# The second network's clamp, square, maximum and rounding issued ahead of the last block product's addition, and no conversions in the first unit

## The chip, the cores and the metric

The kernel runs on one core of one Trainium2 chip. The core has five engines that work side by side, each through its own queue in order: TensorE (PE; its weight loads are shown as PEld), VectorE (DVE), ScalarE (ACT), GpSimd (POOL) and SyncE (SP), which here mostly issues transfers. An engine waits for another through semaphores. The metric is the time of one execution on the device in microseconds, lower is better.

## What is computed

Attention without a softmax, whose output goes through two networks of two layers each:

```python
def _attn_ref(u, v, z):                       # u, v: 2 x 3008 x 256, z: 2 x 3008 x 64
    scores = (1.0 / S) * np.matmul(z, z.transpose(0, 2, 1))
    attn = np.maximum(scores, 0.0) ** 2
    return u * np.matmul(attn, v)

def _moe_ref(x, w_in, w_out):                 # x: 6016 x 256, w_in: 256 x 2048, w_out: 2048 x 256
    h = x @ w_in
    return (h - np.tanh(h)) @ w_out

def _moe2_ref(x, w_in, w_out):                # the same shapes
    h = x @ w_in
    neg, pos = h <= -1.0, h >= 1.0
    g = np.where(pos, h, np.where(neg, 0.0, (h + 1.0) ** 2 / 4.0))
    return g @ w_out
```

The second network's g is the maximum of h and (c/2 + 1/2)^2, where c is h clamped to -1 to 1. The inputs of the networks' weights are 64-bit floats, which the kernel converts itself.

## The kernel before

**Numbers in two parts.** Matrix operands are cut into a rounded part (hi) and the rest (lo); a product of two matrices is three matmuls, hi by lo, lo by hi and hi by hi.

**Stages.** Attention takes some 480 us. Between its steps the weights are converted (`convert`, `posts`, driven by `work`), stored in DRAM (`packed`) and later fetched 512 KB at a time. Then come the units of the first network (net 0, 48 of them), those of the second (net 1, 40), and an end stage for the last tokens of the second network. A unit is one slice of 256 hidden channels (f, 8 of them) for a strip of tokens (s: up to 1024, in two halves of 512).

**One unit** (`Unit.emit`). The first layer is a 2 by 2 block product, done with seven block products instead of eight (`mult`, L557, three matmuls each). They collect in three PSUM banks Y, X and V; intermediate sums in Y are copied out by ScalarE (`snap`: m1, u2, u3) before the next product is added into the same bank. VectorE adds them up (`add`, L496) to the hidden values: half A (`ha`: m1 + X, then u3 + V) and half B (`hb`: a copy of Y by ScalarE, and u2 + V). Each half then goes through the steps of `Half`:

- `first` is the tanh on ScalarE in net 0 (L509) and the clamp on VectorE in net 1 (L511);
- `square` (L516, ScalarE) is there in net 1 alone;
- `value` (L519, VectorE) is the subtraction in net 0 and the maximum in net 1, into `ta` or `tb`;
- `round` (L493 by `copy`, ScalarE) makes the rounded part `gha` or `ghb`;
- `rest` (L530, VectorE) makes the remainder `gla` or `glb`.

The second layer (`parts`, L576) takes these as operands, 24 matmuls a unit. It runs one unit later: while unit u does its first layer, `one`, `two` and `three` of the unit ahead of it, p, stand between the products. `one` needs gha, `two` gla and ghb, `three` glb. So a unit has 21 + 24 = 45 matmuls.

**What sets the order.** Nothing is scheduled: each engine takes its instructions in the order in which `emit` writes them. In net 1 the order before is: round of p's A and clamp of p's B ahead of m1; p's A rest and B square; m1 + X; p's B value; B's rounding; a filling step; u3; u3 + V; **then** p's B rest; a filling step; the clamp of the own A; the products into Y and V; the copy for B; the square of A; the addition for B; the value of A.

**Filling steps.** `fill` is called twice in a unit (once in the first one). It takes the next step of the splitting of the following strip's tokens (`x_steps`, in units f = 2 to 5: subtractions L433, roundings L452, remainders L468), or the turning of finished output (L688), and when there is none, a piece of weight conversion (`work`).

**The last unit of a strip.** `empty`, called at the end of the following unit, copies the four finished banks out; in net 1 all four copies are ScalarE's.

Of the kernel before, what the change touches and what calls it, by code (L numbers as in the profile page):

```python
# [29 lines left out]
def attention_then_two_ffn(  # L30
# [452 lines left out]
    def fill():  # L483

        if fills:
            for fn in fills.pop(0):
                if fn is not None:
                    fn()
        else:
            work(CONVERT[1])  # L490

    def copy(out_, in_):
        nc.scalar.activation(out=out_, in_=in_, func=AF.Copy)  # L493

    def add(out_, x, bank):
        nc.vector.tensor_tensor(out=out_, in0=x, in1=bank, op=ALU.add)  # L496
# [46 lines left out]
    class Unit:  # L543
# [57 lines left out]
        def emit(self, p, att=None):  # L601

            w = self.w
            one, two, three = p.parts_list if p else ([], [], [])
            Y = self.bank()
            self.mult(Y, A11, "b11", True)
            if p and p.net == 1:
                p.A.round()
                p.B.first()
            m1 = self.snap("m1", Y)  # L610
            X = self.bank()
            self.mult(X, A12, "b21", True)
            if p:
                p.A.rest()
                p.B.first() if p.net == 0 else p.B.square()
            self.A = Half(self.net, w, "a")
            add(self.A.h[:, 0, :w], m1, X[:, :w])
            V = self.bank()
            self.mult(V, S1, "t1", True)
            self.mult(Y, S2, "t2")  # L620
            u2 = self.snap("u2", Y)
            if p:
                p.B.value()
            for fn in one:
                fn()
            if att:
                att[0]()
            if p:
                p.B.round()
                fill()  # L630
            self.mult(Y, S3, "t3")
            u3 = self.snap("u3", Y)
            if p and p.net == 0:
                p.B.rest()
            add(self.A.h[:, 1, :w], u3, V[:, :w])
            if p and p.net == 1:
                p.B.rest()
            for fn in two:
                fn()
            if att:  # L640
                att[1]()
            fill()
            if self.net == 1:
                self.A.first()
            self.mult(Y, A22, "t4")
            self.mult(V, S4, "b22")
            self.B = Half(self.net, w, "b")
            if self.net == 0:
                self.A.first()
                copy(self.B.h[:, 1, :w], Y[:, :w])  # L650
                self.A.value()
                add(self.B.h[:, 0, :w], u2, V[:, :w])
            else:
                copy(self.B.h[:, 1, :w], Y[:, :w])
                self.A.square()
                add(self.B.h[:, 0, :w], u2, V[:, :w])
                self.A.value()
            for fn in three:
                fn()
            if self.net == 0:  # L660
                self.A.round()
            if p:
                p.empty()
            self.parts_list = self.parts()
# [58 lines left out]
    def end_s(q):  # L723

        f, c = divmod(q, 2)
        n = SIZES[c]
        xh, xl = xsp[c]
        win = ws[len(units) + f][0]
        banks = [ps_f.tile([P, 512], F32, tag="f", name="h") for _ in range(2)]
        for j in range(2):  # L730
            for k in range(2):
                for i, (wp, x) in enumerate(((0, xl), (1, xh), (0, xh))):
                    nc.tensor.matmul(  # L733
                        banks[j][:, :n], win[wp][:, 2 * k + j, :], x[:, k, :n],
                        start=(k == 0 and i == 0), stop=(k == 1 and i == 2),
                    )
        return banks
# [129 lines left out]
    with tc.manual_schedule():  # L867
# [52 lines left out]
        def work(amount):  # L920

            if not (converts or posts):
                return
            state["credit"] += amount
            if posts:
                cost, fn = posts.pop(0)
                fn()
                state["credit"] -= cost
            while converts and state["credit"] > 0:
                if state["step"] == 0:  # L930
                    next(converts[0])
                elif state["step"] == 4 and len(converts) > 1:
                    next(converts[1])
                state["step"] += 1
                cost = next(converts[0], None)
                if cost is None:
                    converts.pop(0)
                    state["step"] = 1
                else:
                    state["credit"] -= cost  # L940
# [65 lines left out]
        p = None  # L1006
        for i, (net, s, f) in enumerate(units):
# [10 lines left out]
            p = u  # L1018
# [2 lines left out]
        one, two, three = p.parts_list  # L1021
        nq = 2 * NPF
        banks = end_s(0)
        p.A.round()
        p.B.first()
        p.A.rest()
        p.B.square()
# [53 lines left out]
```

## Time and profile before

| | us |
|---|---|
| median of 3 runs (lowest to highest) | 1528.29 (1525.94 to 1530.37) |
| the profiled execution | 1522.68 |
| span in it, first to last instruction | 1520.9 |
| TensorE busy | 1465.9 (96%) |
| VectorE busy | 1264.5 (83%) |
| ScalarE busy | 1034.3 (68%) |
| GpSimd busy | 54.5 (4%) |

The end of a matmul is modelled in these profiles, so that a busy TensorE is not one at its peak; weight loads are the closer measure, as each matmul has one (80% of the span). Times in the trace are counted from the start of the span. In the rows, "<-" in square brackets names what ended an engine's idle time ahead of the instruction, and how long that was.

### The profile page before, as it was taken

What the parts mean: (1) busy time and instruction counts of PE and PEld (TensorE: products, weight loads), DVE (VectorE), ACT (ScalarE), POOL (GpSimd) and SP (SyncE); (2) the same over time, 40 slices, a digit from 0 to 9 for tenths busy, and PEclk for the clock granted to TensorE, in tenths of its full rate; (3) what the DMA queues carried; (4) which work ended last, traced back from release to release, by engine and by line L of the source; (5) the groups of instructions that cost most, each with busy time, mean ns of one, the idle gap of its engine ahead of it and who ended that gap; (6) DMA issues with size and microseconds to landing.
All of it is one profiled execution on the core that took longest, in us unless ns stands there. A gap on an engine that the chain in (4) does not pass through costs nothing.

```text
span 1520.9 us, 22304 instructions
## 1 busy us (share of the span) xinstructions
PE 1465.9 (96%) x8653; PEld 1223.2 (80%) x8653; DVE 1264.5 (83%) x1510; ACT 1034.3 (68%) x1249; POOL 54.5 (4%) x69
## 2 busy tenths in 40 slices
PE   9999999999999999999999999989988899899998
PEld 6888998888888888888888889867776777677897
DVE  8999888988897888888989898777777777777775
ACT  8877778877776677676767767655656556565543
POOL 0110000000110000000000010000000000000000
PEclk9999999999999999999999999999999999999999
DMA  6333335233335657584746575645435645346361
GB/s 153 84 98 98 98 98 115 64 94 95 97 105 178 235 200 252 170 303 135 287 148 247 184 252 206 235 171 192 137 107 161 206 166 165 104 141 211 125 194 25
DMA packets 202170, 240.80 MB, mean 158 GB/s; under 512 B 130000, under 2 KB 139088, under 8 KB 202064
## 3 DMA queue, kind: packets, MB, share of 16 engines
q1 hardware_dynamic: 200864, 239.12, 48.2%
q8 instruction: 67, 1.10, 0.3%
q10 hardware_dynamic: 1200, 0.26, 0.1%
q14 instruction: 39, 0.32, 0.1%
HBM read 195.69 MB, written 43.65 MB: 157 GB/s over the span
## 4 chain that ended last, share of the span: by engine, by line
PE 72%; DVE 12%; ACT 9%; issue 5%; DMA 1%; SPq 0%; ACTq 0%; DVEq 0%
PE acc L335 24%; PE acc L576 21%; PE m L557 17%; PE sc L287 6%; DVE ta L519 3%; ACT ta L516 3%; PE h L733 3%; DVE ha L496 2%; DVE tb L519 2%; DVE glb L530 2%; ACT gha L493 2%; PE acc L769 1%; PE acc L790 1%; DVE ta L511 1%; ACT u L493 1%
## 5 line engine op out<-in xcount | busy, mean ns | idle before, releaser
L335 PE MATMUL acc<-hi,v 64*128 64x512 f32 (+1 forms) x2256 | 282.3, 383 | 0.0
L335 PEld LDWEIGHTS acc<-hi,v 64*128 64x128 f32 x2256 | 220.3, 184 | 35.6 <-ACT hi L300 0.8
L557 PE MATMUL m<-xht,w 128*128 128x512 f32 (+1 forms) x704 | 216.7, 389 | 0.0
L308 ACT ACTIVATE r<-sc 128x1024 f32<-128x1024 f32 (+1 forms) x143 | 143.6, 1004 | 72.4 <-PE sc L287 71.7
L321 DVE TENSOR_TENSOR lo<-a,hi 128x1024 fp32r<-128x1024 f32 (+1 forms) x143 | 171.6, 1207 | 20.3 <-ACT a L315 17.7
L576 PE MATMUL acc<-ghb,w 128*128 128x512 f32 (+1 forms) x704 | 186.5, 387 | 0.0
L557 PE MATMUL m<-xlt,w 128*128 128x512 f32 (+1 forms) x352 | 141.7, 403 | 46.2 <-ACT m L493 46.0
L576 PE MATMUL acc<-gha,w 128*128 128x512 f32 (+1 forms) x704 | 175.2, 392 | 0.0
L576 PEld LDWEIGHTS acc<-gha,w 128*128 128x128 f32 x704 | 133.9, 190 | 27.9
L335 PE MATMUL acc<-lo,v 64*128 64x512 f32 (+1 forms) x1104 | 153.4, 384 | 1.7 <-DVE lo L321 1.7
L576 PEld LDWEIGHTS acc<-ghb,w 128*128 128x128 f32 x704 | 132.2, 188 | 25.9
L557 PEld LDWEIGHTS m<-xht,w 128*128 128x128 f32 x704 | 132.8, 189 | 24.4
L311 ACT ACTIVATE hi<-r 128x1024 fp32r<-128x1024 f32 (+1 forms) x143 | 149.3, 1044 | 4.2
L530 DVE TENSOR_TENSOR gla<-ta,gha 128x1024 fp32r<-128x1024 f32 (+1 forms) x88 | 106.7, 1213 | 44.7 <-ACT gha L493 44.7
L493 ACT ACTIVATE gha<-ta 128x1024 fp32r<-128x1024 f32 (+1 forms) x88 | 92.6, 1052 | 64.3 <-DVE ta L519 63.5
L519 DVE TENSOR_TENSOR ta<-ha,ta 128x1024 f32<-128x1024 f32 (+1 forms) x88 | 107.0, 1216 | 32.6 <-ACT ta L516 19.4
L493 ACT ACTIVATE u<-m 128x512 f32<-128x512 f32 (+1 forms) x176 | 103.7, 589 | 43.9 <-PE m L557 38.5
L317 DVE TENSOR_TENSOR a<-r 128x1024 f32<-128x1024 f32 (+1 forms) x95 | 114.9, 1210 | 21.4 <-ACT r L308 19.2
L557 PEld LDWEIGHTS m<-xlt,w 128*128 128x128 f32 x352 | 66.1, 188 | 76.3 <-ACT m L493 63.8
L493 ACT ACTIVATE ghb<-tb 128x1024 fp32r<-128x1024 f32 (+1 forms) x88 | 92.6, 1052 | 47.9 <-DVE tb L519 47.9
L335 PEld LDWEIGHTS acc<-lo,v 64*128 64x128 f32 x1104 | 108.9, 184 | 19.6 <-DVE lo L321 3.2
L493 ACT ACTIVATE hb<-m 128x512 f32<-128x512 f32 (+1 forms) x88 | 52.2, 594 | 102.0 <-PE m L557 100.8
(103 smaller groups left out, 2435.1 us busy)
## 6 DMA issues: line engine op xcount, KB each, us to landing
w<-packed SPq DMA_DIRECT2D x288, 512.0 KB, 5.7
xr<-kept SPq DMA_DIRECT2D x20, 512.0 KB, 7.7
widein<-in_moe_w_in_dram SPq DMA_DIRECT2D x16, 512.0 KB, 5.8
wideout<-in_moe_w_out_dram SPq DMA_DIRECT2D x16, 512.0 KB, 4.2
packed<-phin SPq DMA_DIRECT2D x16, 512.0 KB, 2.8
packed<-plin SPq DMA_DIRECT2D x16, 512.0 KB, 2.9
vraw<-in_v_dram SPq DMA_DIRECT2D x22, 256.0 KB, 3.7
out_dram<-ot SPq DMA_DIRECT2D x88, 64.0 KB, 1.9
```

Source lines behind the costliest of these rows:

```text
L287: nc.tensor.matmul(ps[:, j, :n], zs[b, g][half, x, k0 : k0 + P], q[half, y, :n], start=(k == 0), stop=(k == 2))
L308: nc.scalar.activation(out=r[s], in_=ps[s], func=AF.Relu)
L311: nc.scalar.activation(out=hi[s], in_=r[s], func=AF.Square)
L317: nc.vector.tensor_tensor(out=a[s], in0=r[s], in1=r[s], op=ALU.mult)
L321: tail.append(lambda: nc.vector.tensor_tensor(out=lo[s], in0=a[s], in1=hi.bitcast(F32)[s], op=ALU.subtract))
L335: nc.tensor.matmul(acc[d][h][:, :n], lhsT, g[half, j, :n], start=start, stop=stop)
L493: nc.scalar.activation(out=out_, in_=in_, func=AF.Copy)
L516: nc.scalar.activation(out=self.t[self.s], in_=self.t[self.s], func=AF.Square, scale=0.5, bias=0.5)
L519: nc.vector.tensor_tensor(out=self.t[self.s], in0=self.h[self.s], in1=self.t[self.s], op=ALU.subtract if self.net == 0 else ALU.max,)
L530: nc.vector.tensor_tensor(out=self.lo[self.s], in0=self.t[self.s], in1=self.hi.bitcast(F32)[self.s], op=ALU.subtract)
L557: nc.tensor.matmul(bank[:, : self.w], self.win[wp][:, block, :], xop[self.net, self.s][x][xp], start=start and i == 0, stop=True, skip_gro ...
L576: nc.tensor.matmul(self.acc(d, n)[:, : self.w], self.wout[:, part, j, d * P : (d + 1) * P], g[:, at, : self.w], start=start, stop=stop,)
```

## The change

In the units of net 1, p's B rest is written directly behind B's rounding and the filling step, ahead of the second addition to A; the own A's clamp directly behind that addition, ahead of `two` and of the second filling step; A's square ahead of the copy for B; A's value ahead of the addition for B. The rounding of A stands at the end of its own unit in both networks, and p's clamp of B behind the product A12. In the first unit of all (the one with `att`, net 0) the tanh of A is written ahead of attention's last steps, and the filling step is left out.

```diff
             Y = self.bank()
             self.mult(Y, A11, "b11", True)
-            if p and p.net == 1:
-                p.A.round()
-                p.B.first()
             m1 = self.snap("m1", Y)
             X = self.bank()
             self.mult(X, A12, "b21", True)
             if p:
+                if p.net == 1:
+                    p.B.first()
                 p.A.rest()
                 p.B.first() if p.net == 0 else p.B.square()
...
             if p:
                 p.B.round()
                 fill()
+                p.B.rest()
             self.mult(Y, S3, "t3")
             u3 = self.snap("u3", Y)
-            if p and p.net == 0:
-                p.B.rest()
             add(self.A.h[:, 1, :w], u3, V[:, :w])
-            if p and p.net == 1:
-                p.B.rest()
+            if self.net == 1 or att:
+                self.A.first()
             for fn in two:
                 fn()
             if att:
                 att[1]()
-            fill()
+            if not att:
+                fill()
             if self.net == 1:
-                self.A.first()
+                self.A.square()
             self.mult(Y, A22, "t4")
             self.mult(V, S4, "b22")
             self.B = Half(self.net, w, "b")
-            if self.net == 0:
+            if self.net == 0 and not att:
                 self.A.first()
-                copy(self.B.h[:, 1, :w], Y[:, :w])
-                self.A.value()
-                add(self.B.h[:, 0, :w], u2, V[:, :w])
-            else:
-                copy(self.B.h[:, 1, :w], Y[:, :w])
-                self.A.square()
-                add(self.B.h[:, 0, :w], u2, V[:, :w])
-                self.A.value()
+            copy(self.B.h[:, 1, :w], Y[:, :w])
+            self.A.value()
+            add(self.B.h[:, 0, :w], u2, V[:, :w])
             for fn in three:
                 fn()
-            if self.net == 0:
-                self.A.round()
+            self.A.round()
             if p:
                 p.empty()
...
         nq = 2 * NPF
         banks = end_s(0)
-        p.A.round()
         p.B.first()
```

VectorE, from the second unit of net 1 into the third, in the kernel before (`ha<-u` is the second addition to A, `hb<-u` the addition for B, `ha<-m` the first addition to A of the next unit):

```order
L519 TENSOR_TENSOR tb<-hb,tb 128x1024
L496 TENSOR_TENSOR ha<-u_11097,m 128x512
L530 TENSOR_TENSOR glb<-tb,ghb 128x1024
L511 TENSOR_SCALAR ta<-ha 128x1024
L496 TENSOR_TENSOR hb<-u_11077,m 128x512
L519 TENSOR_TENSOR ta<-ha,ta 128x1024
L511 TENSOR_SCALAR tb<-hb 128x1024
L530 TENSOR_TENSOR gla<-ta,gha 128x1024
L496 TENSOR_TENSOR ha<-m_11145,m 128x512
```

The same place in the changed kernel:

```order
L519 TENSOR_TENSOR tb<-hb,tb 128x1024
L530 TENSOR_TENSOR glb<-tb,ghb 128x1024
L496 TENSOR_TENSOR ha<-u_11099,m 128x512
L511 TENSOR_SCALAR ta<-ha 128x1024
L519 TENSOR_TENSOR ta<-ha,ta 128x1024
L496 TENSOR_TENSOR hb<-u_11077,m 128x512
L511 TENSOR_SCALAR tb<-hb 128x1024
L530 TENSOR_TENSOR gla<-ta,gha 128x1024
L496 TENSOR_TENSOR ha<-m_11143,m 128x512
```

Two pairs have changed places: glb with the second addition to A, and the value of A (`ta<-ha,ta`) with the addition for B. The clamp of A stands directly behind the addition that it reads, and so does the clamp of B.

ScalarE at the same place, before (`hb<-m` is the copy for B, `ta<-ta` A's square, `m` and `u` are the copies m1, u2 and u3):

```order
L493 ACTIVATE u_11097<-m 128x512
L493 ACTIVATE hb<-m 128x512
L516 ACTIVATE ta<-ta 128x1024
L493 ACTIVATE gha<-ta 128x1024
L493 ACTIVATE m_11145<-m 128x512
L516 ACTIVATE tb<-tb 128x1024
```

And in the changed kernel:

```order
L493 ACTIVATE u_11099<-m 128x512
L516 ACTIVATE ta<-ta 128x1024
L493 ACTIVATE hb<-m 128x512
L493 ACTIVATE gha<-ta 128x1024
L493 ACTIVATE m_11143<-m 128x512
L516 ACTIVATE tb<-tb 128x1024
```

The square has passed the copy for B; the rounding gha stands directly ahead of m1 in both, though it is written in another unit.

VectorE in the first unit of net 0, behind the last sums of attention, before (`y` are these sums, `ut` their scaling; L203 and L205 belong to a weight conversion):

```order
L376 TENSOR_TENSOR y<-y,acc_6171 128x448
L379 SCALAR_TENSOR_TENSOR ut_5_6535<-y,ut_5_6535 128x2x448
L203 TENSOR_SCALAR ein_1_6532<-ein_1_6532 128x512
L205 SCALAR_TENSOR_TENSOR min_1_6531<-widein_1_5960,min_1_6531 128x512
L519 TENSOR_TENSOR ta<-ha,ta 128x1024
```

And in the changed kernel:

```order
L376 TENSOR_TENSOR y<-y,acc_6171 128x448
L379 SCALAR_TENSOR_TENSOR ut_5_6535<-y,ut_5_6535 128x2x448
L519 TENSOR_TENSOR ta<-ha,ta 128x1024
L496 TENSOR_TENSOR hb<-u_6611,m 128x512
```

The two conversions have moved to a later unit, and every conversion behind them moves by one filling step.

## Rows read from the trace of the kernel before

**Rows 1.** Waits, 960 to 1425 us: in total, times, longest us.

```profile
PEld m L557 <- ACT m L493: 60.9, 40, 2.5
DVE glb L530 <- ACT ghb L493: 0.4, 1, 0.4
```

**Rows 2.** Weight loads' busy us in a stretch, count, granted clock, DMA share, GB/s.

```profile
966.00:1431.00 465.00, 335.92 (x1800) 1.00 0.50 165
```

**Rows 3.** Timeline, starts of units: start, duration us, engine, line, operation.

```profile
504.76 0.19 PEld L557 LDWEIGHTS m<-xlb,w 128*128 128x128 f32 x1
514.96 0.19 PEld L557 LDWEIGHTS m<-xlb,w 128*128 128x128 f32 x1
...
966.30 0.19 PEld L557 LDWEIGHTS m<-xlb,w 128*128 128x128 f32 x1
...
1431.52 2.68 PEld L733 LDWEIGHTS h<-xe,w 128*128 128x128 f32 x12
```

**Rows 4.** Timeline, one unit of the second network and what leads to it.

```profile
1203.83 1.06 ACT L493 ACTIVATE ghb<-tb 128x1024 fp32r<-128x1024 f32 x1 [0.89 <-DVE tb L519]
1204.80 1.04 ACT L452 ACTIVATE xht<-t 128x1024 fp32r<-128x1024 f32 x1
1205.74 0.58 ACT L493 ACTIVATE u<-m 128x512 f32<-128x512 f32 x1
1206.35 0.69 DVE L496 TENSOR_TENSOR ha<-u,m 128x512 f32<-128x512 f32 x1 [1.42 <-ACT u L493]
1206.95 1.22 DVE L530 TENSOR_TENSOR glb<-tb,ghb 128x1024 fp32r<-128x1024 f32 x1
...
1208.09 0.68 DVE L433 TENSOR_TENSOR t<-xr,t 128x512 f32<-128x512 f32 x1
1208.69 0.69 DVE L511 TENSOR_SCALAR ta<-ha 128x1024 f32<-128x1024 f32 x1
...
1209.41 0.19 PEld L557 LDWEIGHTS m<-xlb,w 128*128 128x128 f32 x1
...
1209.47 1.06 ACT L516 ACTIVATE ta<-ta 128x1024 f32<-128x1024 f32 x1 [1.02 <-DVE ta L511]
...
1210.57 1.23 DVE L519 TENSOR_TENSOR ta<-ha,ta 128x1024 f32<-128x1024 f32 x1 [0.59 <-ACT ta L516]
...
1211.83 1.06 ACT L493 ACTIVATE gha<-ta 128x1024 fp32r<-128x1024 f32 x1 [1.29 <-DVE ta L519]
1212.79 0.58 ACT L493 ACTIVATE m<-m 128x512 f32<-128x512 f32 x1
1212.92 1.23 DVE L530 TENSOR_TENSOR gla<-ta,gha 128x1024 fp32r<-128x1024 f32 x1 [0.52 <-ACT gha L493]
...
1213.42 0.19 PEld L557 LDWEIGHTS m<-xlt,w 128*128 128x128 f32 x1 [2.01 <-ACT m L493]
...
1214.06 0.68 DVE L496 TENSOR_TENSOR ha<-m,m 128x512 f32<-128x512 f32 x1
...
1214.42 0.60 ACT L493 ACTIVATE u<-m 128x512 f32<-128x512 f32 x1
1214.65 1.22 DVE L519 TENSOR_TENSOR tb<-hb,tb 128x1024 f32<-128x1024 f32 x1
```

**Rows 5.** Timeline, ScalarE's copies of a finished strip in the second network.

```profile
1069.52 2.05 ACT L493 ACTIVATE y<-acc 128x512 f32<-128x512 f32 x4
```

**Rows 6.** Timeline, first unit of the first network and the start of the next.

```profile
488.90 1.39 DVE L376 TENSOR_TENSOR y<-y,acc 128x448 f32<-128x448 f32 x2 [0.54 <-ACT y L375]
...
489.53 1.05 ACT L509 ACTIVATE ta<-ha 128x1024 f32<-128x1024 f32 x1
...
490.32 1.09 DVE L379 SCALAR_TENSOR_TENSOR ut<-y,ut 128x896 f32<-128x896 f32 x1
...
492.27 1.22 DVE L519 TENSOR_TENSOR ta<-ha,ta 128x1024 f32<-128x1024 f32 x1
...
495.11 0.20 PEld L557 LDWEIGHTS m<-xlt,w 128*128 128x128 f32 x1 [2.42 <-ACT m L493]
```

## The prediction, made before the changed kernel had run

> **What bounds the kernel now.** I read the waits of the last long stage first. Between 960 and 1425 us TensorE's weight loader sits idle 40 times, 60.9 us in all, until ScalarE has copied the product m1 out of its bank [rows 1]; no other wait ends an idle of TensorE there. Forty is the number of second-network units, one wait in each. The second view is the busy time of that stage: 1800 weight loads in 465 us, at a granted clock of 1.00 [rows 2]. 1800 is 40 times 45, the products of a unit.
>
> The third view is where units begin. In the first network one unit begins 10.20 us after the other (504.76, 514.96), which is 45 loads of 0.227 us without a gap: that is TensorE's own pace. In the second network the units run from 966.30 to 1431.52, 465.2 us, or 11.63 each [rows 3]. At 10.20 they would need 408.0, and some 0.6 less since the first unit still finishes 24 products of 448 columns: 407.4. **57.8 us are lost there**, and these are all that a better order can give back in that network.
>
> The fourth view is one such unit row by row [rows 4]. It begins at 1209.41. The tenth load writes the bank that m1 is copied from, and was due at 1209.41 + 9 x 0.227 = 1211.45; it comes at 1213.42, 0.05 after the copy m1 ended. The copy was free to start at about 1210.6, when its product was ready. It started at 1212.79, because on ScalarE it stands behind the rounding of the A half (gha), which waits for VectorE's value (ta<-ha,ta), which waits for ScalarE's square, which waits for VectorE's clamp. The clamp started at 1208.69, although its input was complete at 1207.04: VectorE did glb and one operation of the token splitting first.
>
> **The change, part by part: the order in the second network.** No operation is added or removed there; on VectorE glb goes ahead of the second addition to A, the clamp directly behind that addition, and the value ahead of the addition for B; on ScalarE the square goes ahead of B's copy. First the same unit again, from its measured start: glb could start behind ghb (1203.83 + 1.06 + 0.03 = 1204.92). The addition ha<-u keeps 1206.35, since u3 ends then. The clamp follows at 1206.35 + 0.69 + 0.03 = 1207.07, 1.6 earlier than now. The square starts 0.69 + 0.09 later, 1207.85, and takes 1.06; the value 1208.95, the rounding 1210.21, m1 0.96 behind it at 1211.17, TensorE goes on at 1211.17 + 0.58 + 0.05 = 1211.80. The wait of 1.97 is down to 0.35 [rows 4].
>
> But the next units do not start from that state, because glb now stands in the chain. Its input ghb comes late, so **VectorE gets a new wait**: today glb waits for ghb 0.4 us in the whole stage [rows 1]; afterwards some 1.1 in each unit (1.06 + 0.03), and the addition, the clamp and all behind them queue after it. VectorE and ScalarE then form a ring that goes round once per unit without TensorE. Its length, in durations of [rows 4] (start to start where neighbours are independent, 1.14 for 1.22; end plus 0.03 where one reads what the other wrote): clamp 0.69 + 0.09, square 1.06 + 0.04, value 1.14, addition for B 0.71, clamp of B 0.61, gla 1.14, first addition 0.59, value of B 1.22 + 0.04, ghb 1.06 + 0.03, glb 1.14, second addition 0.71. The sum is **10.27 us, against TensorE's 10.20**. The filling work of VectorE lies under ScalarE's square (1.06) and under ghb, and costs nothing while it is one operation at each place.
>
> Between two dependent VectorE neighbours I take a price from rows of the first unit: the scaling starts at 490.32, 0.03 after the two additions that it reads ended (488.90 + 1.39) [rows 6], while independent neighbours overlap by 0.09 (1212.92 + 1.23 against 1214.06) [rows 4]. The change makes two dependent pairs (addition to clamp, in A and in B), so 0.24 of the ring is this. The Trainium skill, page "VectorE: DVE Perf Modes", section "The DRAIN you can't avoid", says that the next operation waits for the pipe to empty anyway and that a semaphore between two costs nothing extra; by it the ring would be 10.03 and hide under TensorE. The rows do not bear it out here: they differ by 0.12 with and without the dependence.
>
> What is left of the 57.8 us then: (a) 40 x 0.07 = 2.8 from the ring. (b) In units where the token splitting puts a 1.04 us rounding (xht) between ghb and u3, u3 sets the addition: 0.97 + 0.94 + 0.58 + 0.03 = 2.52 after ghb's start instead of 1.06 + 0.03 + 1.14 = 2.23. That is 0.29 in 14 units (three in each of four strips, two for the last tokens): 4.1. (c) In four units the copies of finished output, 2.05 us for four [rows 5], stand between the rounding of A and m1, which then is about 1.9 late and nearly all of it is waited for: 4 x 1.95 = 7.8; after each, VectorE and ScalarE are ahead by some 0.4, which absorbs part of (a) and (b): -1.7. Together 13.0 remain, and **57.8 - 13.0 = 44.8 us go**.
>
> **The first unit of the first network.** Its filling step goes, which issued two conversions on VectorE between the scaling and the value of A (490.32 + 1.09 to 492.27, about 0.9 us [rows 6]). In exchange the tanh (1.05) now stands ahead of the two copies of attention's last sums, so the additions, the scaling and what follows are about 1.0 later. The wait that both feed, 2.42 at 495.11 [rows 6], moves by 0.1; bounds are -1 and +1 (either of the two without the other). I take 0. The conversions themselves, and their stores on SyncE's queue, come half a unit later to the end of the network; TensorE has no wait on them in the stage before, and the next network's last weights are fetched several units afterwards, so 0. In the first network the other operations keep their order on each engine. The end stage starts from an earlier gha, but TensorE does not wait there now: 0.
>
> **The sum.** The profiled execution took 1522.68 us, of which 1520.9 are the span; minus 44.8 it would be 1477.9. The runs have a median of 1528.29, 0.4% above the profiled one, so I forecast 1528.3 - 44.8 = 1483.5, about **1483 us**.
>
> **The rivals.** *The ring stays under TensorE's 10.20* (the dependent pairs cost nothing, ring 10.03): (a) goes, (b) shrinks to about 0.5, (c) stays near 7; 7.5 remain, 1478 us. For it: the handovers of 0.03 are already short. Against: the rows on dependent pairs. *The ring is longer*: if the four cheap handovers between the two engines (0.03 to 0.04) cost the 0.09 that the square waits after the clamp, it is 10.51, and 40 x 0.24 = 9.6 more remain: 1493. For it: every 0.1 us counts 4 us, and nothing in the trace runs this ring end to end. *It doesn't do what it says*: TensorE's wait only moves, to the product that needs the second addition, for that addition now stands behind glb and its bank is due 36 loads (8.16 us) after the unit's start, with the addition done at about 7.7 to 8.0. That costs more than forecast only when the ring is long; it eats the whole gain, within 0.3% of today, at a ring of 11.5 to 11.7, 1.3 above mine. *Slower*: the same place, from a ring of 11.75 on. If VectorE's wait for ghb were 1.7 longer than worked, the ring would be 12.0 and the kernel 1528 + 40 x (12.0 - 11.63) = 1543. It would need B's rounding held up by ScalarE's copy u2 in front of it. Against it: the way through TensorE (m1 0.58 + 0.05, product to u2 1.00, u2 0.60, ghb and the ring from there to m1, 7.0) adds up to 9.2, less than 10.2 [rows 4].
>
> **How the numbers follow.** Forecast 0.50; shorter ring 0.20 (1478); longer ring 0.24 (1493); wait only moved 0.03; slower 0.03. Measurements of this kernel tell about 0.3%, 4.6 us, from no change: faster by more than that 0.94, within it 0.03, slower 0.03. The range takes in the shorter ring less the 1 us of the first unit and the scatter of the runs (1528.29 - 1525.94 = 2.4), and the longer ring with as much: 1474 to 1496.
>
> **What would show it.** Right: second-network units begin 10.2 to 10.6 apart; the sum of TensorE's waits for m1 falls from 60.9 to under 20, with four of about 2 us; glb waits for ghb some 1.1 us in each unit, 40 us and more in all; the first network stays at 10.20. Wrong: units at 11 us or more, waits of TensorE that end with the second addition (ha<-u) or with u3, or a first network that is slower.

## The result

| | before | changed |
|---|---|---|
| median of 4 runs (lowest to highest), us | 1527.12 (1523.62 to 1530.37) | 1481.22 (1480.46 to 1481.43) |
| the profiled execution, us | 1522.68 | 1480.46 |
| span in it, us | 1520.9 | 1478.6 |
| mean granted clock of TensorE in it | 0.997 | 0.999 |

The ratio is 0.970 (95% interval 0.968 to 0.972): the changed kernel is faster by 45.9 us between the medians and by 42.3 us between the spans. Forecast were 1483 us, with 1474 to 1496 as the range.

Where the 42.3 us of span went, by the starts of units in both traces:

| stretch | before, us | changed, us | difference |
|---|---|---|---|
| attention, up to the first unit | 480.40 | 479.89 | -0.5 |
| the first two units of net 0 | 24.36 | 22.63 | -1.7 |
| the other 46 units of net 0 | 461.54 | 462.26 | +0.7 |
| the 40 units of net 1 | 465.22 | 424.42 | -40.8 |
| end stage | 89.38 | 89.40 | 0.0 |

So nearly all of it comes from the second network, as forecast. What is left there is in the waits of the changed kernel between 960 and 1380 us (engine, line, what it waited for: us in total, times, longest):

```profile
ACT ta L516 <- DVE ta L511: 70.6, 39, 2.2
ACT ghb L493 <- DVE tb L519: 37.7, 39, 1.3
...
DVE glb L530 <- ACT ghb L493: 24.2, 31, 1.1
PEld m L557 <- ACT m L493: 20.3, 31, 2.3
```

TensorE still waits for m1 (and once, for 0.18 us, for ghb), but for 20.3 us where it was 60.9 [rows 1]. No wait of the weight loader for the second addition or for u3 has come in its place. VectorE now waits for ghb, 24.2 us where it was 0.4. The busy times of the whole kernel have hardly moved (the page's first part):

```profile
PE 1457.6 (99%) x8653; PEld 1236.3 (84%) x8653; DVE 1267.5 (86%) x1510; ACT 1030.1 (70%) x1249; POOL 55.5 (4%) x69
```

Weight loads fill 84% of a shorter span. In the second network, as the windows show it (stretch, its us, busy us, loads, granted clock, DMA share, GB/s), there are the same loads as in [rows 2], but for two at the edges, in 424.7 us:

```profile
964.50:1389.20 424.70, 335.58 (x1802) 1.00 0.54 183
```

The stretch begins and ends with these rows of the timeline, which answer to the last two of [rows 3]:

```profile
964.78 0.19 PEld L557 LDWEIGHTS m<-xlb,w 128*128 128x128 f32 x1
...
1389.20 2.68 PEld L726 LDWEIGHTS h<-xe,w 128*128 128x128 f32 x12
```

Of the 57.8 us that the prediction found lost in this network, 424.4 - 407.4 = 17.0 remain, against 13.0 forecast. By the starts of its 40 units: 16 last 10.29 to 10.48 us (2.9 us in all over 10.20 each), 12 last 10.62 to 10.80 (5.5 us; eleven of them have a rounding of the token splitting between ghb and u3, the other is the second), four behind the copies of finished output last 12.30 to 12.33 (8.5 us), and eight run at TensorE's own pace, 10.20 or less.

**The ring, row by row.** This is the timeline of the changed kernel through one round, from one value of A to the next (start us, duration us, engine, line, operation; in brackets the idle time ahead and what ended it):

```profile
1155.46 1.23 DVE L519 TENSOR_TENSOR ta<-ha,ta 128x1024 f32<-128x1024 f32 x1 [0.57 <-ACT ta L516]
...
1156.60 0.68 DVE L496 TENSOR_TENSOR hb<-u,m 128x512 f32<-128x512 f32 x1
...
1157.39 0.69 DVE L511 TENSOR_SCALAR tb<-hb 128x1024 f32<-128x1024 f32 x1
...
1158.00 1.22 DVE L530 TENSOR_TENSOR gla<-ta,gha 128x1024 fp32r<-128x1024 f32 x1
...
1159.14 0.68 DVE L496 TENSOR_TENSOR ha<-m,m 128x512 f32<-128x512 f32 x1
...
1159.74 1.22 DVE L519 TENSOR_TENSOR tb<-hb,tb 128x1024 f32<-128x1024 f32 x1
...
1160.99 1.06 ACT L493 ACTIVATE ghb<-tb 128x1024 fp32r<-128x1024 f32 x1 [0.72 <-DVE tb L519]
...
1162.08 1.23 DVE L530 TENSOR_TENSOR glb<-tb,ghb 128x1024 fp32r<-128x1024 f32 x1 [0.50 <-ACT ghb L493]
...
1163.22 0.68 DVE L496 TENSOR_TENSOR ha<-u,m 128x512 f32<-128x512 f32 x1
1163.94 0.69 DVE L511 TENSOR_SCALAR ta<-ha 128x1024 f32<-128x1024 f32 x1
...
1164.72 1.06 ACT L516 ACTIVATE ta<-ta 128x1024 f32<-128x1024 f32 x1 [1.91 <-DVE ta L511]
...
1165.82 1.23 DVE L519 TENSOR_TENSOR ta<-ha,ta 128x1024 f32<-128x1024 f32 x1 [0.57 <-ACT ta L516]
```

The round takes 1165.82 - 1155.46 = **10.36 us**, without a row that waits for TensorE. Start to start the steps are 1.14, 0.79, 0.61, 1.14, 0.60, 1.25, 1.09, 1.14, 0.72, 0.78, 1.10. The prediction had 1.14, 0.71, 0.61, 1.14, 0.59, 1.26, 1.09, 1.14, 0.71, 0.78, 1.10 and a sum of 10.27. One step is off by more than 0.01: from the addition for B to the clamp of B, 0.79 where 0.71 was put down. The clamp of B starts 0.11 after the addition ended; the clamp of A starts 0.04 after its own (1163.22 + 0.68).

### The profile page after: what moved, and what is told of

Its sections match the earlier page's. It is cut to its first block, busy times and chain, and to the rows that moved or that the text cites. A ratio compares the mean times of both kernels' runs of the same rounds, so it can differ in the third digit from the quotient of the medians.

```text
span 1478.6 us, 22265 instructions
## 1 busy us (share of the span) xinstructions
PE 1457.6 (99%) x8653; PEld 1236.3 (84%) x8653; DVE 1267.5 (86%) x1510; ACT 1030.1 (70%) x1249; POOL 55.5 (4%) x69
## 4 chain that ended last, share of the span: by engine, by line
PE 75%; DVE 14%; ACT 7%; issue 2%; DMA 1%; SPq 1%; ACTq 0%; DVEq 0%
PE acc L335 24%; PE acc L576 21%; PE m L557 19%; PE sc L287 6%; PE h L726 3%; DVE ta L519 2%; DVE ha L496 2%; ACT ta L516 2%; DVE tb L519 2%; DVE gla L530 2%; PE acc L762 1%; DVE glb L530 1%; DVE ta L511 1%; ACT ghb L493 1%; PE acc L783 1%
## 5 line engine op out<-in xcount | busy, mean ns | idle before, releaser
L335 PEld LDWEIGHTS acc<-hi,v 64*128 64x128 f32 x2256 | 228.5, 184 | 27.0 <-ACT hi L300 0.8
L530 DVE TENSOR_TENSOR glb<-tb,ghb 128x1024 fp32r<-128x1024 f32 (+1 forms) x88 | 106.9, 1214 | 33.0 <-ACT ghb L493 32.6
L335 PEld LDWEIGHTS acc<-lo,v 64*128 64x128 f32 x1104 | 112.8, 184 | 15.6 <-DVE lo L321 3.2
L519 DVE TENSOR_TENSOR tb<-hb,tb 128x1024 f32<-128x1024 f32 (+1 forms) x88 | 106.5, 1210 | 5.3 <-ACT tb L516 1.0
```

Of the source, the lines that this page charges most:

```text
L335: nc.tensor.matmul(acc[d][h][:, :n], lhsT, g[half, j, :n], start=start, stop=stop)
L519: nc.vector.tensor_tensor(out=self.t[self.s], in0=self.h[self.s], in1=self.t[self.s], op=ALU.subtract if self.net == 0 else ALU.max,)
L530: nc.vector.tensor_tensor(out=self.lo[self.s], in0=self.t[self.s], in1=self.hi.bitcast(F32)[self.s], op=ALU.subtract)
```

## The experiments

Theory: VectorE and ScalarE go round once per unit without TensorE, each of the moved operations shortens that round, and its length is what a unit takes. Rivals: one of the moves alone does the work and the others lie under TensorE; or the first unit of the first network has a share in the gain. The ratios are to the kernel before on the same chip, with their 95% intervals. Its medians beside the runs are 1525.5 to 1527.1 us, so a difference in us between two kernels below holds to some 2 us.

**Undo one move: glb behind the second addition again.**

```diff
                 p.B.round()
                 fill()
-                p.B.rest()
+                if p.net == 0:
+                    p.B.rest()
...
             add(self.A.h[:, 1, :w], u3, V[:, :w])
+            if p and p.net == 1:
+                p.B.rest()
```

> The changed kernel with one step undone: in the second network glb stands behind the second addition to A again, ahead of the clamp of A. Ring theory (what the chain from the second addition to A over clamp, square, value, rounding to the copy m1 takes, queue by queue, sets TensorE's wait, and a ring of VectorE and ScalarE sets its floor): the clamp is 1.1 to 1.6 us later again in every unit; going through the units with the durations of the rows, TensorE's waits for m1 are 0.5 to 0.6 in plain units and 1.1 to 1.6 in units with token splitting, 41 us lost in all instead of 15: 1481 + 26 = 1507 us. Rival (the square and the value ahead of the addition for B are what helps, glb's place does not matter): 1481 to 1484 us.

Measured: 1511.87 us (1510.08 to 1512.95), ratio 0.990 (0.989 to 0.992). Of the gain two thirds are gone. The waits between 960 and 1420 us:

```profile
PEld m L557 <- ACT m L493: 47.5, 39, 2.6
```

Now every unit but the first waits for m1, by 0.56 to 0.64 us in plain units and by 1.58 behind a long rounding, since u3, which ScalarE copies behind ghb and behind that rounding, stands in the ring. The rival (this move does nothing) is out. The time is 5 above the expectation, and in three units of the profile the clock fell as the next run shows it, 1.4 to 1.6 us each.

**Undo one move: the value of A behind the addition for B.**

```diff
             copy(self.B.h[:, 1, :w], Y[:, :w])
-            self.A.value()
+            if self.net == 0:
+                self.A.value()
             add(self.B.h[:, 0, :w], u2, V[:, :w])
+            if self.net == 1:
+                self.A.value()
```

> The changed kernel with the value of A behind the addition for B again (second network). Ring theory: VectorE holds the value back until the last block product is there, 0.53 us of wait in every unit instead of 0.26 to 0.57 in some and none in others; 25 us lost instead of 15: 1481 + 10 = 1491 us, with units at 10.6 us throughout. Rival (value ahead of the addition is the main part of the gain): 1510 us or more.

Measured: 1496.61 us (1496.17 to 1497.53), ratio 0.981 (0.979 to 0.982). The wait for m1 is 0.52 in plain units instead of some 0.28: 15 us more over all. The rival (1510 us or more) is out. But it is 5 over the expectation. The trace says where these are; the timeline has a wait of 2.46 behind the copies of finished output and the start of the next unit, and the windows the stretches around it:

```profile
1061.11 0.19 PEld L557 LDWEIGHTS m<-xlb,w 128*128 128x128 f32 x1
...
1065.58 0.19 PEld L557 LDWEIGHTS m<-xlt,w 128*128 128x128 f32 x1 [2.46 <-ACT m L493]
1075.29 0.19 PEld L557 LDWEIGHTS m<-xlb,w 128*128 128x128 f32 x1
```

```profile
1059.00:1063.50 4.50, 3.41 (x19) 1.00 0.00 0
1063.50:1067.50 4.00, 1.60 (x7) 0.86 0.00 0
1067.50:1071.50 4.00, 3.10 (x14) 0.71 0.10 16
```

Behind the wait the granted clock is down to 0.86 and 0.71 in these stretches, a part of each at the lower of the two levels (1.2 of 2.4 GHz), and the unit lasts 14.18 us (1061.11 to 1075.29), where 10.20 plus the wait are some 12.6. All four units of this kind do that in this profile: 4 x 1.6 = 6.4 us. In the changed kernel the four waits are 2.21 to 2.26 and the clock stays at 1.00 behind each.

**Undo one move: the square behind the copy for B.**

```diff
-            if self.net == 1:
-                self.A.square()
             self.mult(Y, A22, "t4")
...
             copy(self.B.h[:, 1, :w], Y[:, :w])
+            if self.net == 1:
+                self.A.square()
             self.A.value()
```

> The changed kernel with the square of A behind ScalarE's copy for B again (second network). Ring theory: the square waits for the copy, which waits for TensorE's product into Y, so the chain now runs through TensorE: 0.83 us of wait in every unit, 35 us lost instead of 15: 1481 + 20 = 1501 us, units at 10.9 us. Rival (the copy is short, 0.6 us, and lies beside other work): 1481 to 1485 us.

Measured: 1506.50 us (1505.97 to 1508.12), ratio 0.987 (0.986 to 0.989). Waits between 960 and 1415 us:

```profile
DVE ta L519 <- ACT ta L516: 55.1, 40, 2.1
ACT gha L493 <- DVE ta L519: 51.1, 40, 1.3
PEld m L557 <- ACT m L493: 43.3, 39, 3.1
```

VectorE waits twice as long for the square as in the changed kernel (27.6 us there), and m1 is 0.87 late in each plain unit: the copy for B, which waits for a product of TensorE, stands in the ring. The rival (1481 to 1485 us) is out. The time is again 5 over the expectation; in two of the four units behind the copies (waits of 2.8 to 3.1) the clock fell, and they last 14.5 and 14.8 us where the waits alone make 12.9 and 13.2. That is 3.2 of it in the profiled run.

This run also bears on the step that the ring had wrong. VectorE's order is that of the changed kernel, and yet the clamp of B follows the addition for B within 0.04 (1154.64 + 0.68, then 1155.36):

```profile
1154.64 0.68 DVE L496 TENSOR_TENSOR hb<-u,m 128x512 f32<-128x512 f32 x1
...
1155.36 0.69 DVE L511 TENSOR_SCALAR tb<-hb 128x1024 f32<-128x1024 f32 x1
```

**Shorten the ring: the maximum of half B left out** in the second network (where h exceeds 1 the values are then not the reference's; VectorE has 40 operations of 1.22 us less).

```diff
-            if p:
+            if p and p.net == 0:
                 p.B.value()
...
         p.B.square()
-        p.B.value()
```

> The changed kernel without the maximum of half B in the second network (the maximum with h is left out there, half B goes on with the square alone). Ring theory: the ring of VectorE and ScalarE that goes round once per unit is shorter by 1.2 us, 9.1 instead of 10.35, and so lies under TensorE's 10.20; the waits of 0.26 to 0.57 go in all units, only the four behind the copies of a finished strip stay, at 1.5 instead of 2.2: 1481 - 10 = 1471 us, units at 10.20. Rival (the remaining waits come from the chain inside a unit, from u3 to m1, which has no value of B in it): 1480 to 1482 us, with the same waits.

Measured: 1470.15 us (1469.34 to 1470.77), ratio 0.963 (0.962 to 0.965). Waits between 960 and 1375 us:

```profile
DVE glb L530 <- ACT ghb L493: 48.7, 40, 1.8
PEld m L557 <- ACT m L493: 6.4, 5, 1.4
```

All units run at 10.20 but the first ones and the four behind the copies (11.5). An operation that TensorE never waits for directly was what held it up, and the rival (the chain from u3 to m1, which has no value of B in it) is out: the ring is shown as the bound from this side too. That it is the order, and not only the amount of work, which is less here, the reordered kernel below tells.

**The second network's part alone**, with the first unit of net 0 as it was:

```diff
-            if self.net == 1 or att:
+            if self.net == 1:
                 self.A.first()
...
-            if not att:
-                fill()
+            fill()
...
-            if self.net == 0 and not att:
+            if self.net == 0:
                 self.A.first()
```

> The changed kernel without its part in the first unit: the tanh of A and the filling step stand there as before. Clock theory (the profile of before shows TensorE's granted clock at half in 495 to 499 us, after its wait of 2.42 us, and the profile of the changed kernel, where that wait is split in 1.36 and 1.50, does not): the second unit begins its second layer at the half clock again, 1.6 us dearer, while some 0.7 us of new waits near the end of the first network go, since the conversions keep their places: 1482 us, +0.9. Rival (the first unit's part is worth nothing, as predicted): within 0.5 of 1481.2. The comparison can just tell these apart; the profile's starts of units in the first network can for certain: 12.8 or 14.5 us for the second unit.

Measured: 1482.29 us (1481.46 to 1483.39), ratio 0.972 (0.970 to 0.974). The interval overlaps that of the whole change. In its profile the second unit of net 0 lasts 14.31 us (12.78 in the changed kernel), and net 1 takes 426.1 us where it was 424.4, all of that in its first two units, of which more below.

**The first unit's part alone**, put into the kernel before:

```diff
             add(self.A.h[:, 1, :w], u3, V[:, :w])
+            if att:
+                self.A.first()
...
-            fill()
+            if not att:
+                fill()
...
             if self.net == 0:
-                self.A.first()
+                if not att:
+                    self.A.first()
```

> The kernel before with the part in the first unit alone; the second network keeps its old order. Clock theory: 1.7 us less in the first two units, 0.7 more near the end of the first network: 1526 - 1 = 1525 us, units of the second network as before, 57 us lost there, with some of its waits of 2.5 us followed by a stretch at the half clock, 1.6 us each, in a number that differs from run to run (so several us of scatter). Rival (part of the gain of 45 us comes from the first unit and the later conversions): under 1520 us.

Measured: 1525.23 us (median of 12 runs) against 1525.46 (17 runs), ratio 1.000 (0.999 to 1.001): no difference that can be told, though 2 us either way could hide in it. The rows of TensorE in the second unit are, with the old first unit (the run with the second network's part alone) and with the new one (the first unit's part alone):

```profile
492.09 0.19 PEld L557 LDWEIGHTS m<-xlt,w 128*128 128x128 f32 x1 [0.58 <-ACT hb L493]
495.05 0.29 PEld L557 LDWEIGHTS m<-xlt,w 128*128 128x128 f32 x1 [2.42 <-ACT m L493]
504.50 0.19 PEld L557 LDWEIGHTS m<-xlb,w 128*128 128x128 f32 x1
```

```profile
493.70 0.19 PEld L557 LDWEIGHTS m<-xlt,w 128*128 128x128 f32 x1 [1.36 <-ACT hb L493]
495.72 0.29 PEld L557 LDWEIGHTS m<-xlt,w 128*128 128x128 f32 x1 [1.49 <-ACT m L493]
505.24 0.19 PEld L557 LDWEIGHTS m<-xlb,w 128*128 128x128 f32 x1
```

One wait of 2.42 has become two of nearly the same sum (0.58 + 2.42 = 3.00, 1.36 + 1.49 = 2.85), and the next unit starts 9.45 and 9.52 us behind the second of them. In both profiles the clock fell in this unit, which lasts 14.31 and 14.22 us: splitting the wait does not prevent it, against the clock theory of both expectations.

**A better place for glb: behind the clamp of A**, so that it leaves the ring, alone and together with the filling steps.

```diff
                 p.B.round()
                 fill()
-                p.B.rest()
+                if p.net == 0:
+                    p.B.rest()
...
             if self.net == 1 or att:
                 self.A.first()
+            if p and p.net == 1:
+                p.B.rest()
```

> The changed kernel with glb directly behind the clamp of A in the second network, and nothing else moved: the filling steps stay where they are. Ring theory: VectorE no longer stands waiting for ghb ahead of the second addition, so plain units have no wait for m1 and the four big waits fall from 2.2 to 1.45; but in units with token splitting both filling steps and glb now stand between the second addition and the value, and glb comes after TensorE wants it: 0.2 to 0.7 of wait for glb and 0.5 for m1 there. Going through the units: 21 us lost instead of 15, 1481 + 6 = 1487 us. Rival (VectorE's wait for ghb is the cost, wherever the filling stands): 1472 to 1475 us.

Measured: 1487.63 us (1487.14 to 1488.57), ratio 0.975 (0.973 to 0.976), 6 slower than the change as it is, as expected; the rival is out. Waits of TensorE between 960 and 1395 us:

```profile
PEld m L557 <- ACT m L493: 18.1, 23, 1.5
PEld acc L576 <- DVE glb L530: 9.1, 17, 0.7
```

The wait for m1 is not gone, and there is a new one, for glb itself. The likely reason is the first filling step, whose rounding on ScalarE still lies ahead of u3 as in [rows 4], with the addition, the clamp and glb behind that. The next kernel moves it, together with the second filling step; which of the two matters was not tried alone.

With it, the first filling step behind u3 and the second behind the addition for B, in net 1:

```diff
                 p.B.round()
-                fill()
-                p.B.rest()
+                if self.net == 0:
+                    fill()
+                if p.net == 0:
+                    p.B.rest()
             self.mult(Y, S3, "t3")
             u3 = self.snap("u3", Y)
+            if p and self.net == 1:
+                fill()
...
                 self.A.first()
+            if p and p.net == 1:
+                p.B.rest()
...
-            if not att:
+            if not att and self.net == 0:
                 fill()
...
             add(self.B.h[:, 0, :w], u2, V[:, :w])
+            if self.net == 1:
+                fill()
```

> Ring theory used for a new order in the second network: glb directly behind the clamp of A (under ScalarE's square, so that VectorE doesn't stand waiting for ghb), the first filling step behind u3 instead of ahead of it, the second behind the addition for B. Going through the units with the durations of the rows: no wait in 35 units, 0.2 to 0.5 in the unit behind the splitting, four waits of 1.45 behind the copies of a finished strip; 5.5 us lost instead of 15: 1471 to 1472 us. Rival (what is left is VectorE's and ScalarE's amount of work, not its order): 1480 to 1482 us.

Measured: 1473.01 us (1471.62 to 1473.81), ratio 0.966 (0.964 to 0.968). Between 960 and 1378 us there is this left:

```profile
PEld m L557 <- ACT m L493: 6.9, 5, 1.5
```

Plain units are at 10.20, four wait 1.53 behind the copies. The rival (the amount of work) is out, for no operation is missing here. The filling work has to go where neither engine's part of the ring stands behind it; with that, moving glb pays.

**The four copies of finished output shared**, two on VectorE, alone:

```diff
-                    if d and self.net == 0:
+                    if d:
```

> The changed kernel with two of the four copies of a finished strip on VectorE in the second network. Ring theory: the four waits behind the copies fall from 2.2 to 1.2, but VectorE, which is in the ring, takes 1.2 us more there and gives half of that back in the units behind: 1481 - 2 = 1479 us. Rival (the copies on ScalarE are the whole of these four waits): four times 2.0 less, 1473 us.

Measured: 1480.69 us (1479.88 to 1481.57), ratio 0.970 (0.969 to 0.972). The four waits fall from 2.2 to 1.25, but all units but the first wait now, 39 in place of 31 (19.6 us between 960 and 1385, where it was 20.3): what ScalarE gives off, the ring takes up. The rival (1473 us) is out. In the profile net 1 is 2.1 us shorter (422.3), as expected; from the change as it is the time can't be told.

**Both together**, the reordered kernel with the copies shared:

> As the reordered kernel, and of the four copies of a finished strip in the second network two go to VectorE, as they do in the first network. Ring theory: the copies stand in front of m1 on ScalarE, two instead of four make its wait 0.5 instead of 1.45, four times: 1471.5 - 3 = 1468 us. Rival (the copies on VectorE hold up the clamp of B and with it the ring by as much): 1471 to 1472 us.

Measured: 1469.09 us (1467.74 to 1470.64), ratio 0.963 (0.961 to 0.965), the fastest of all, 12 below the change as it is. The interval overlaps that of the reordered kernel without this; in the profiles net 1 takes 410.6 us where it took 414.7, one less in each of the four units, as expected. The waits between 960 and 1375 us:

```profile
PEld m L557 <- ACT m L493: 3.0, 5, 0.7
PEld acc L576 <- ACT ghb L493: 1.6, 6, 0.4
```

**The same with the first unit's filling step kept**, behind the addition for B:

```diff
-            if self.net == 1:
+            if self.net == 1 or att:
                 fill()
```

> The reordered kernel with shared copies, and in the first unit of the first network the filling step is kept, behind the addition for B, so that all conversions and their transfers stand in their old places. Transfer theory (the conversions that come half a unit later put their loads and stores on the queue ahead of the fetch of the next tokens near the end of the first network; VectorE waits 2 to 3 us for it instead of 1.15, and TensorE 0.5 to 1.5 us for VectorE): that wait near 917 us is gone, VectorE's wait for the tokens is about 1.2 again; 1469 - 1 = 1468 us. Rival (the wait there is chance, it differs from run to run): the same wait of 0.5 to 1.5 us.

Measured: 1469.88 us (1468.72 to 1470.21), ratio 0.963 (0.962 to 0.965): no difference that can be told. This run was to settle a wait in the last units of net 0. VectorE's first subtraction for the next strip (`t<-xr,xr`) needs tokens that SyncE fetches; before, in the changed kernel and in this one (timeline):

```profile
916.49 0.69 DVE L433 TENSOR_TENSOR t<-xr,xr 128x512 f32<-128x512 f32 x1 [1.15 <-DMA xr<-kept]
```

```profile
915.18 0.69 DVE L433 TENSOR_TENSOR t<-xr,xr 128x512 f32<-128x512 f32 x1 [2.10 <-DMA xr<-kept]
...
917.46 0.50 PEld L557 LDWEIGHTS m<-xhc,w 128*128 128x128 f32 x3 [0.49 <-DVE ha L496]
```

```profile
916.16 0.69 DVE L433 TENSOR_TENSOR t<-xr,xr 128x512 f32<-128x512 f32 x1 [1.51 <-DMA xr<-kept]
...
918.44 0.51 PEld L557 LDWEIGHTS m<-xhc,w 128*128 128x128 f32 x3 [0.26 <-DVE ha L496]
```

SyncE's queue explains most of it. Before, the two stores of converted weights and the load of the next ones (`packed`, `wideout`, issued 898.17 to 900.42) had gone out ahead of the fetch, which was issued at 906.79 and was used 9.70 later. With half a unit's delay they are issued directly behind it (fetch at 904.92, the three at 906.41 to 907.93) and share the DMA engines with it: used 10.26 later. The load, which landed 3.6 us after its issue, now takes 9.8. With the old first unit the delay is 9.61, with the filling step kept 10.05; in four other kernels with the new first unit (the first unit's part alone, the reordered one, the copies shared, both together) it is 10.45 to 11.36, and TensorE waits up to 1.58 (the reordered kernel with shared copies).

So with the step kept most of the wait is gone, as the transfer theory has it, but not all (10.05 against 9.61 and 9.70). It took 1.3 us off TensorE's wait, and 1.7 came back elsewhere: the first two units of net 1 take 22.5 us where they took 20.8, with waits of 1.31 and 1.60 for m1. The first of them is due to a rounding of converted weights on ScalarE, ahead of a tanh that m1 stands behind. In the old place it waits for the store of the rounding before it, 2.8 to 2.9 us in all three kernels that have the conversions there; half a unit later it waits for nothing. Before and changed:

```profile
965.56 0.63 ACT L230 ACTIVATE phout<-wout 128x512 fp32r<-128x512 f32 x1 [2.77 <-DMA packed<-phin]
...
969.68 0.19 PEld L557 LDWEIGHTS m<-xlt,w 128*128 128x128 f32 x1 [1.40 <-ACT m L493]
```

```profile
969.37 0.62 ACT L230 ACTIVATE phout<-wout 128x512 fp32r<-128x512 f32 x1
```

## Why the prediction was right, and where it was not

**The loss and its place: right in the main.** TensorE's waits for m1 were what could be won, and nearly all of the gain is theirs. But not all of the 57.8 us were for the new order to give back. One unit of that stage lasted 14.20 us in the profile of before, where others of its kind take 12.6, because the clock fell in it (below): 1.6 us. And the first unit's wait of 1.40 came from a conversion, not from the order: with the new order alone that unit still lasts 11.03 us.

**The chain through VectorE and ScalarE: right, one step short.** That the round becomes the bound, and not TensorE, is shown by two kernels: without B's maximum, and with glb and the filling work out of the round, plain units run at 10.20 and the kernel is 8 to 11 us faster, with the same work for TensorE. The three undone moves each bring a product of TensorE back into the round (u3, the last block product, the copy for B) and cost 15 to 31 us. Together that is 71 us of a gain of 46: the moves have no shares that add up.

The step that failed is "Between two dependent VectorE neighbours I take a price from rows of the first unit". For the addition and clamp of A it held (0.03 to 0.04); for B it is 0.11, so the round is 10.36 and not 10.27. In the program B's clamp reads what two engines wrote (VectorE's addition and ScalarE's copy for the other rows of `hb`), A's what VectorE alone wrote. The kernel with the square behind the copy tells more. There VectorE has waited for the square just before, and so for the copy ahead of it on ScalarE; the clamp of B follows the addition in 0.03 to 0.04 in all 35 units between 960 and 1375 us where they are neighbours, against 0.10 to 0.11 in 35 of 37 in the changed kernel. So the 0.07 hang on the copy's place behind the square. A second wait, for ScalarE, is the likely reason; the trace does not show a wait that is over at once.

The Trainium skill, "VectorE: DVE Perf Modes", section "The DRAIN you can't avoid", finds that a semaphore between two operations costs nothing extra, on a row of eight copies. These rows do not bear that out: a start comes 0.08 to 0.09 before the end of an independent neighbour, 0.03 to 0.04 after that of one which is waited for, and 0.11 after in the case of B.

**What is left: 17.0 for 13.0.** Terms (a), (b) and the slack were put at 2.8 + 4.1 - 1.7 = 5.2 and are 2.9 + 5.5 = 8.4. The step that failed accounts for this: with a round of 10.36, (a) is 40 x 0.16 = 6.4 and the three come to 8.8. Term (b) had its 0.29 right (10.36 + 0.29 = 10.65, and these units last 10.62 to 10.70), in 11 units where it was put in 14. Term (c) was put at 4 x 1.95 = 7.8 and is 8.5, 2.12 each. The slack behind these four units is as described: two units run at 10.20 behind each but the first (one there).

**The first unit: put at 0, and no more can be told.** The two orders start the next product at nearly the same time, and the kernel with this part alone has a ratio of 1.000, to 0.001 either way. Of the 1.7 us that the two profiles show in the second unit, 1.4 are the clock and not the order: with the new first unit it lasts 14.22 us where the clock fell and 12.78 where it did not.

**The conversions half a unit later: put at 0, and wrong twice.** I looked for who needs the converted weights and not at whose transfers their stores and loads meet. That is the +0.7 in the other units of net 0. Nor did I look at what waits for their stores: the first unit of net 1 lasts 9.69 us instead of 10.90 since ScalarE's rounding no longer does, so 1.2 of the 40.8 us won there are this. That the two nearly cancel is luck.

**What the sum had not at all is the clock.** From its own execution the prediction gives 1522.68 - 44.8 = 1477.9, and the profiled run of the changed kernel took 1480.46: the sum is 2.6 too good. Between the medians it is 1.1 too poor (44.8 against 45.9). The runs of before lie 8.6 us apart, from 1520.77 at a mean clock of 0.998 to 1529.38 at 0.993 (17 runs, those beside the parts alone); the four of after lie within 1 us, all at 0.999. From the fastest of these to the median of after it is 39.5 us; and of the 42.3 between the two spans, 39.3 are left without the two falls of the clock in the profile of before (1.4 in the second unit of net 0, 1.6 in net 1). So by estimate some 39 us are the change's, and 6 to 7 more the clock's. Two errors of the prediction, a gain put too high and a clock left out, nearly cancel in the medians, and that 1483 came so near to 1481 is luck in this part. How the 6 to 7 divide over the units was not measured.

**Its signs.** Units 10.2 to 10.6 apart: 10.2 to 10.8, but for the four of 12.3. Waits for m1 under 20 with four of about 2: 20.3, with four of 2.2. VectorE's wait for ghb at 40 or more: 24.2, which misses, since a filling operation often lies where the wait would be, as the prediction had said of it elsewhere. The first network at 10.20: but for the one wait. Of the rivals, the ring under TensorE's 10.20 and the one of 10.51 lie on either side of the measured 10.36, and in net 1 nothing of TensorE waits for the second addition.

## What to carry to other kernels

Where two engines in order feed each other, add up their steps once round, from handover to handover: if the sum exceeds the pace of the engine that you want to keep busy, it is the floor, even if neither of the two is busy all the time (here 86% and 70%), and an operation is worth what it adds to that round. Filling work is not free where a step of the round stands behind it; here its place, not its amount, decided whether moving one more operation lost 6 us or won 8. And of a step that is moved, look at whose transfers its own will meet, and at who waits for them.

## What the hardware showed beside that

Waits of TensorE cost more than their length where the granted clock falls behind them. In the windows of weight loads in the profile of before, the stretch after the wait of 2.42 in the second unit of net 0 [rows 6], and one after a wait of 2.52 in net 1:

```profile
495.00:497.00 2.00, 1.50 (x6) 0.56 0.89 307
497.00:499.00 2.00, 1.57 (x6) 0.59 1.02 416
```

```profile
1331.00:1335.00 4.00, 2.82 (x10) 0.57 0.83 330
1335.00:1339.00 4.00, 3.32 (x18) 1.00 0.44 129
```

The same place in the changed kernel, which begins 2 us earlier, with nine and ten loads where there were six:

```profile
495.00:497.00 2.00, 1.65 (x9) 1.00 0.99 352
497.00:499.00 2.00, 1.65 (x10) 1.00 1.00 393
```

Means of 0.56 to 0.59 are mostly the lower of the two levels, 1.2 GHz. Each such fall costs 1.4 to 1.6 us. It does not come behind every long wait: in net 1 of before, four others of 2.50 to 2.55 were not followed by one, with the value put back all four of 2.46 were, and in the second unit of net 0 it came in two of two profiles with the old first unit and in six of eleven with the new one. What decides it stays open here. In the profiles it accounts for 4.7, 6.4 and 3.2 of the some 5 us by which the three kernels with a move undone came out over their expectation, and is the likely reason why the time of the kernel before scatters more than that of the changed one.
